# Agent attention with a mixture of experts: the marking of tokens that need their own answer, and the checked columns of the next batch

## The chip, the cores and the metric

The kernel runs on one core of one Trainium2 chip. The metric is the device time of one execution in microseconds (us). Two kernels are told apart here by medians of several executions. The engines are called as in the profile: PE multiplies matrices (PEld loads its weights), DVE, ACT and POOL work on vectors, and SP only issues transfers between device memory and the chip's own memory, one after the other in the order of its queue.

## The reference

Four batches of 11456 tokens with 128 values each go through attention over 49 agents per batch. The result of that is routed, token by token, to the one of 8 experts whose embedding is nearest, and gated.

```python
def sm(a, b):
    s = scale * (a @ b.transpose(0, 2, 1))
    s = s - s.max(-1, keepdims=True)
    e = np.exp(s)
    return e / (e.sum(-1, keepdims=True) + 1e-09)
agent_v = sm(agents, k) @ v
x = (sm(q, agents) @ agent_v).reshape(B * S, D)
...
logits = xn @ en.T / tau
expert_idx = np.argmax(logits, axis=1)
gate_w = probs[np.arange(N), expert_idx]
for e in range(E):
    mask = expert_idx == e
    h = np.maximum(x[mask] @ w1[e], 0.0)
    out[mask] = gate_w[mask, None] * (h @ w2[e])
```

## The kernel before, in words

The kernel does each batch in units of 8 columns of 128 tokens. A first pass over k and v builds the batch's agent values; a second pass over q computes scores, weights, routing and the answer. Nearly all tokens of a batch go to one expert, so the kernel picks that expert per batch (`pick_expert`) and computes its answer for all tokens in one cheap form: a linear part (`yp` from `lin`, L1275) plus two blocks of hidden columns (`hp`, `hh`, `hl`, and `yp` from `w2p`, L1284 to L1286), added up in PSUM. DVE multiplies the finished `yp` by the gate into a tile `ot` (L1299), and SP writes that to the output (L1306). There are three `ot` tiles; a fourth one waits until the transfer of the first has landed.

The cheap form treats most hidden columns as always on or always off. The hidden columns nearest to a change of sign are the checked columns: `pick_expert` gathers them into `vm` at its very end (L936), and `proved` (L1127 to L1133) multiplies every token with them and keeps a minimum and a sum. `mark_strays(b)` then finds the tokens whose answer is not covered: those whose own expert is another one, whose scale is out of bounds, or whose check failed. It builds a one-hot of the best expert (`oh`), its index (`idx`), bounds (`odd`, `ne`), the candidate list (`mine`), waits until all columns are checked, and takes the top candidates of each partition (`top`, `some`, `had`, `mput`), all as small DVE steps with a few PE products between. Up to 128 of a batch's marked tokens are answered exactly by `fix(b)`, which loads an expert's weights (`w1s`, `w2s`, L945 and L946), gathers the tokens, computes (`sqT`, `ssp`, `seT`, `sx`, `shp`, `syp`) and scatters the answers into the output (L1396). Left-over tokens are counted and handled in a loop (`stray`).

The program is written by Python generators that take turns; `yield n` hands over for n turns. `mark_strays(b)` is started when the last group of the batch is routed, and `fix(b)` waits until `vm` of the next batch exists. What the generators write is not yet the order of an engine: a scheduler places each instruction by when it expects the data and the engine, among those written nearby. Each engine then runs its own list strictly in order, and SP's list too: a transfer that waits (for its data, or for the transfer eight places earlier in the list, whose completion semaphore it uses) holds up all behind it. In batch 3, where no batch follows, marking and fixing run as urgent work at the end.

Of the kernel before, what the change touches and what calls it, by code (L numbers as in the profile page):

```python
# [11 lines left out]
F32 = mybir.dt.float32  # L12
# [3 lines left out]
ALU = mybir.AluOpType  # L16
AX = mybir.AxisListType
ROP = bass.bass_isa.ReduceOp

P = 128  # L20
# [10 lines left out]
def kernel(ctx: ExitStack, tc: tile.TileContext, q, k, v, agents, emb, tau, w1, w2, out):  # L31
    nc = tc.nc
    pe, dve, act, pool, sp = nc.tensor, nc.vector, nc.scalar, nc.gpsimd, nc.sync

    B, N, C = q.shape
    A = agents.shape[1]
    E, D, F = w1.shape
# [14 lines left out]
    NCOL = J + REM_J  # L52
# [30 lines left out]
    sm = ctx.enter_context(tc.tile_pool(name="sm", bufs=2))  # L83
# [208 lines left out]
    down = cst.tile([P, E], F32, name="down")  # L292
# [93 lines left out]
    batches = [Obj() for _ in range(B)]  # L386
# [659 lines left out]
    def route_group(b, gi, n):  # L1046
# [67 lines left out]
        if gi == len(groups) - 1:  # L1114
            spawn(mark_strays(b) if b < B - 1 else urgent(mark_strays(b), 4), 1, half=True)
# [27 lines left out]
    def mark_strays(b):  # L1143

        bt = batches[b]
        while bt.groups < len(groups):
            yield 1
        odd = sm.tile([P, NCOL], F32, name="odd", tag="odd", bufs=1)
        ne = sm.tile([P, NCOL], F32, name="ne", tag="ne", bufs=1)
        dve.tensor_tensor(out=ne, in0=bt.l, in1=bt.l, op=ALU.mult)  # L1150
# [2 lines left out]
        yield 1  # L1153
        ga = gate_all[:, b, :]
        dve.tensor_scalar(ga, bt.es, 1e-9, None, ALU.add)
        oh = bt.lg
        dve.scalar_tensor_tensor(out=oh, in0=bt.lg, scalar=0.0, in1=down.unsqueeze(1).broadcast_to([P, NCOL, E]),
                                 op0=ALU.is_equal, op1=ALU.mult)
        yield 1
        dve.reciprocal(ga, ga)  # L1160
        yield 1
        idx = sm.tile([P, NCOL], F32, name="idx", tag="idx", bufs=1)
        dve.tensor_reduce(out=idx, in_=oh, axis=AX.X, op=ALU.max)
        yield 1
        dve.tensor_scalar(ne, idx, bt.e0, None, ALU.not_equal)
        yield 1
# [23 lines left out]
        for i in range(KEEP):  # L1190
# [5 lines left out]
                          in1=had[:, :KEEP].unsqueeze(2).broadcast_to([P, KEEP, P]), op=ALU.is_equal)  # L1196
# [505 lines left out]
    with nullcontext():  # L1702
        due = []
        for i in range(len(ticks) + LAG):
            if i < len(ticks):
                b, t, r = ticks[i]
# [12 lines left out]
            while due and due[0][0] <= i:  # L1719
                _, b, t, f = due.pop(0)  # L1720
# [44 lines left out]
```

## Time and profile before

| | before |
|---|---|
| median of 3 runs | 677.67 us (677.25 to 678.22) |
| profiled execution, own time | 679.16 us |
| its span, from first to last instruction | 677.4 us |
| mean granted TensorE clock | 0.986 |
| PE busy | 632.3 us, 93% of the span |
| DVE busy | 525.1 us, 78% |
| ACT busy | 478.3 us, 71% |
| POOL busy | 317.7 us, 47% |
| transfers on the main queue | 68.8% of 16 engines' span |

The own time of the profiled execution is 1.49 us above the median of the runs and 1.8 us above its span. PE is the busiest engine by far; its idle time, and the stretches in which it was granted half of its clock, are what the other engines and the transfers cost.

### The profile page before, as it was taken

The page shows a single profiled execution, that of the slowest core. Times are in us where ns is not written, and L with a number is a line of the kernel's source. Part 1 is how long each engine was busy: PE and PEld are TensorE (multiplying, and loading weights), DVE is VectorE, ACT ScalarE, POOL GpSimd, SP SyncE. Part 2 cuts the span into 40 slices and gives each one's busy share as a digit, 9 for nine tenths or more (in the row PEclk, how much of TensorE's full clock was granted, in tenths as well). Part 3 has the DMA queues.
Part 4 walks back from the last instruction along what each step waited for, and adds up shares of the span by engine and source line. Part 5 has one row for each costly group of instructions (what it writes and reads, how often), then busy time and mean ns, then how long its engine had stood idle before and what let it go on. Part 6 is the DMA issues. An engine that isn't in the chain of part 4 may idle for free. (4 is left out here: it accounts for less than half of the span.)

```text
span 677.4 us, 23627 instructions
## 1 busy us (share of the span) xinstructions
PE 632.3 (93%) x9309; PEld 524.3 (77%) x9309; DVE 525.1 (78%) x1483; ACT 478.3 (71%) x1362; POOL 317.7 (47%) x588
## 2 busy tenths in 40 slices
PE   8998999999998899999999797999999999999995
PEld 6887788778886787888877586687887778887784
DVE  4757988867678999776779985986576999958992
ACT  3556589887689757887779753876657974888831
POOL 6000455375406536874524412677463356867300
PEclk9998999999999999999999997999999999999998
DMA  8998389989986399797986277739585534244121
GB/s 338 295 302 298 117 191 253 216 189 276 227 213 158 101 218 265 188 233 205 289 251 152 78 151 204 182 101 265 138 251 159 141 104 129 49 112 129 64 97 41
DMA packets 163138, 124.81 MB, mean 184 GB/s; under 512 B 82860, under 2 KB 139264, under 8 KB 163026
## 3 DMA queue, kind: packets, MB, share of 16 engines
q1 hardware_dynamic: 162706, 123.01, 68.8%
q8 instruction: 74, 1.21, 0.7%
q0 software_dynamic: 320, 0.27, 0.2%
q14 instruction: 38, 0.31, 0.1%
HBM read 80.26 MB, written 23.79 MB: 154 GB/s over the span
## 5 line engine op out<-in xcount | busy, mean ns | idle before, releaser
L1261 DVE SCALAR_TENSOR_TENSOR hl<-hp,hh 128x512 f16<-128x512 f32 (+1 forms) x184 | 122.3, 667 | 30.9 <-ACT hh L1260 30.1
L1284 PE MATMUL yp<-w2p,hh 128*128 128x128 f16 x720 | 137.4, 219 | 3.1 <-ACT hh L1260 2.9
L1285 PE MATMUL yp<-w2p,hh 128*128 128x128 f16 x720 | 136.8, 219 | 0.0
L1131 ACT ACTIVATE under<-vp 128x304 f16<-128x304 f32 (+1 forms) x268 | 114.8, 429 | 29.2 <-PE vp L1127 25.2
L1260 ACT ACTIVATE hh<-hp 128x512 f16<-128x512 f32 (+1 forms) x184 | 107.4, 589 | 37.9 <-PE hp L1257 29.4
L1286 PE MATMUL yp<-w2p,hl 128*128 128x128 f16 x720 | 133.6, 219 | 0.4 <-DVE hl L1261 0.4
L440 ACT COPY fT<-fTp 128x512 f32<-128x512 f32 (+1 forms) x136 | 75.4, 574 | 28.7 <-PE fTp L433 18.6
L1127 PE MATMUL vp<-vm,tt 128*128 128x304 f16 x360 | 93.0, 293 | 1.9 <-ACT under L1131 0.5
L451 PEld LDWEIGHTS sp<-aT_all,fT 128*64 128x64 f32 x2336 | 78.9, 139 | 17.5 <-issue 7.8
L451 PE MATMUL sp<-aT_all,fT 128*64 128x49 f32 x2336 | 89.4, 226 | 1.7 <-ACT fT L440 0.6
L1284 PEld LDWEIGHTS <-hh 128*128 128x128 f16 x720 | 71.3, 99 | 17.8 <-ACT hh L1260 5.7
L994 POOL TENSOR_TENSOR e<-qe,e 128x392 f16<-128x392 f32 (+1 forms) x46 | 40.5, 880 | 84.4 <-ACT e L993 80.8
L1286 PEld LDWEIGHTS <-hl 128*128 128x128 f16 x720 | 71.0, 99 | 11.2 <-issue 1.5
L1299 DVE TENSOR_TENSOR ot<-yp,gs 128x512 f32<-128x512 f32 (+1 forms) x92 | 61.5, 670 | 17.9 <-DMA out_dram<-ot 9.2
L1285 PEld LDWEIGHTS <-hh 128*128 128x128 f16 x720 | 70.8, 98 | 5.3 <-issue 0.5
L1256 PE MATMUL hp<-tt,gh 128*128 128x512 f16 (+1 forms) x184 | 69.0, 376 | 3.2 <-ACT under L1131 1.3
L1275 PE MATMUL yp<-lin,tt 128*128 128x128 f16 x720 | 62.6, 220 | 8.1 <-DVE ot L1299 7.8
L1078 POOL TENSOR_TENSOR nrm<-qq,half 128x16 f32<-128x16 f32 (+2 forms) x28 | 69.8, 2492 | 0.0
L1257 PE MATMUL hp<-tt,gl 128*128 128x512 f16 (+1 forms) x184 | 68.9, 375 | 0.0
L1275 PEld LDWEIGHTS <-tt 128*128 128x128 f16 x720 | 48.9, 99 | 13.4 <-issue 4.9
L1131 ACT ACTIVATION_READ_ACCUMULATOR under<-vp 128x1 f32 (+1 forms) x268 | 55.4, 207 | 0.0
L433 PE MATMUL fTp<-ident,qt 128*128 128x128 f32 (+1 forms) x344 | 54.5, 281 | 0.7 <-ACT under L1131 0.3
(366 smaller groups left out, 1513.4 us busy)
## 6 DMA issues: line engine op xcount, KB each, us to landing
kt<-in_k_dram SPq DMA_DIRECT2D x44, 512.0 KB, 7.0
vt<-in_v_dram SPq DMA_DIRECT2D x44, 512.0 KB, 5.7
out_dram<-ot SPq DMA_DIRECT2D x88, 256.0 KB, 2.7
qt<-in_q_dram SPq DMA_DIRECT2D x42, 512.0 KB, 6.1
w1s<-in_moe_w_dram SPq DMA_DIRECT2D x9, 512.0 KB, 4.1
w2s<-in_moe_w_dram SPq DMA_DIRECT2D x9, 512.0 KB, 8.2
q<-in_q_dram SPq DMA_DIRECT2D x2, 512.0 KB, 11.0
tt<-e SPq DMA_TRANSPOSE x46, 3.1
```

The lines of the kernel that those rows point to most:

```text
L440: act.copy(dst, tp[:, : m * p])
L451: i = pe.matmul(out=s[h : h + w, c * A : (c + 1) * A], lhsT=xT[:, c * p + h : c * p + h + w], rhs=rhs, start=True, stop=True, skip_group_c ...
L1078: pool.tensor_tensor(out=nrm, in0=quad, in1=half[:, :n], op=ALU.pow)
L1127: pe.matmul(out=z[:p, :FV], lhsT=tts[b, u][:, c * p : (c + 1) * p], rhs=bt.vm, start=True, stop=True)
L1131: act.activation(under[:p], z[:p, :FV], AF.Relu, scale=-1.0, accum_out=bt.vsum[:p, at])
L1256: pe.matmul(out=hp[:, :m], lhsT=bt.gh[:, fs], rhs=tt, start=True, stop=False)
L1260: h_last[:] = [act.activation(hh[:, :m], hp[:, :m], AF.Relu)]
L1261: dve.scalar_tensor_tensor(out=hl[:, :m], in0=hp[:, :m], scalar=0.0, in1=hh[:, :m], op0=ALU.max, op1=ALU.subtract)
L1275: pe.matmul(out=yp[:p, c, :], lhsT=tc_, rhs=bt.lin[:, h], start=(c == 0 and h == 0), stop=False, skip_group_check=True)
L1284: pe.matmul(out=y, lhsT=hh[:, cs], rhs=wh, start=False, stop=False, skip_group_check=True)
L1285: pe.matmul(out=y, lhsT=hh[:, cs], rhs=wl, start=False, stop=False, skip_group_check=True)
L1286: y_last[:] = [pe.matmul(out=y, lhsT=hl[:, cs], rhs=wh, start=False, stop=last, skip_group_check=True)]
```

## The change

In `mark_strays`, the one-hot `oh` and the index `idx` are written first, as soon as all groups of the batch are routed. For batches 0 to 2 a wait follows in the writing order, until the next batch's `vm` has been written, and two turns more; the bounds, the candidates, the top search, the scatter positions, the gates and the counts are written after it. For batch 3 only the order of the first steps changes. No instruction is added or taken away.

```diff
         while bt.groups < len(groups):
             yield 1
+        oh = bt.lg
+        dve.scalar_tensor_tensor(out=oh, in0=bt.lg, scalar=0.0, in1=down.unsqueeze(1).broadcast_to([P, NCOL, E]),
+                                 op0=ALU.is_equal, op1=ALU.mult)
+        yield 1
+        idx = sm.tile([P, NCOL], F32, name="idx", tag="idx", bufs=1)
+        dve.tensor_reduce(out=idx, in_=oh, axis=AX.X, op=ALU.max)
+        yield 1
+        if b < B - 1:
+            while not hasattr(batches[b + 1], "vm"):
+                yield 1
+            yield 2
         odd = sm.tile([P, NCOL], F32, name="odd", tag="odd", bufs=1)
         ne = sm.tile([P, NCOL], F32, name="ne", tag="ne", bufs=1)
         dve.tensor_tensor(out=ne, in0=bt.l, in1=bt.l, op=ALU.mult)
...
         dve.tensor_scalar(ga, bt.es, 1e-9, None, ALU.add)
-        oh = bt.lg
-        dve.scalar_tensor_tensor(out=oh, in0=bt.lg, scalar=0.0, in1=down.unsqueeze(1).broadcast_to([P, NCOL, E]),
-                                 op0=ALU.is_equal, op1=ALU.mult)
-        yield 1
         dve.reciprocal(ga, ga)
-        yield 1
-        idx = sm.tile([P, NCOL], F32, name="idx", tag="idx", bufs=1)
-        dve.tensor_reduce(out=idx, in_=oh, axis=AX.X, op=ALU.max)
         yield 1
```

After the change, lines from about L1176 on stand 4 lines lower (L1306 is L1310, L1192 is L1196). The listings below are of what the scheduler made of each program.

The first place is where the next batch's `vm` is made, in the marking of batch 1. This is SP's list there, before: the loads `vt` (v of the next pass) and `w2s` (weights for `fix`), the transpose `kT`, another `vt`, then the outputs of finished `ot` tiles.

```order
L159 DMA vt_8418<-in_v_dram 128x8x128
L946 ISA
L946 DMA w2s_8523<-in_moe_w2_dram 128x8x128
L555 DMA_TRANSPOSE kT_8361<-ks_8124 128x16x128
L159 DMA vt_8544<-in_v_dram 128x8x128
L1306 DMA out_0_dram<-ot_8407 128x512
L1306 DMA out_0_dram<-ot_8563 128x512
L1306 DMA out_0_dram<-ot_8671 96x256
L1306 DMA out_0_dram<-ot_8778 128x512
```

And the same place of SP's list after the change:

```order
L159 DMA vt_8406<-in_v_dram 128x8x128
L159 DMA vt_8521<-in_v_dram 128x8x128
L555 DMA_TRANSPOSE kT_8354<-ks_8121 128x16x128
L1310 DMA out_0_dram<-ot_8396 128x512
L946 ISA
L946 DMA w2s_8577<-in_moe_w2_dram 128x8x128
L1310 DMA out_0_dram<-ot_8536 128x512
L1310 DMA out_0_dram<-ot_8666 96x256
L1310 DMA out_0_dram<-ot_8768 128x512
```

The second `vt` has moved ahead of the transpose, the first output stands right behind the transpose, and `w2s` has moved from ahead of the transpose to behind that output. On DVE the same place reads so before, with `vm`, the `ot` that needs the first of these outputs landed, and the marking's `had` and `mput`:

```order
L936 TENSOR_SCALAR vm_7312<-placed_8235,thr_8206 128x304
L1299 TENSOR_TENSOR ot_8778<-yp_8707,gs_8108 128x512
L982 TENSOR_REDUCE qmx_8332<-sp_8315 128x8
L985 TENSOR_TENSOR qe_8334<-sp_8315,qmx_8332 128x392
L1192 TENSOR_SCALAR had_8358<-iotaf_147,had_8379 128x3
L1195 TENSOR_TENSOR mput_8416<-iotaf_147,had_8358 128x384
```

And after the change:

```order
L1303 TENSOR_TENSOR ot_8768<-yp_8703,gs_8106 128x512
L936 TENSOR_SCALAR vm_7312<-placed_8224,thr_8199 128x304
L982 TENSOR_REDUCE qmx_8328<-sp_8311 128x8
L985 TENSOR_TENSOR qe_8330<-sp_8311,qmx_8328 128x392
L1265 SCALAR_TENSOR_TENSOR hl_8736<-hp_8732,hh_8735 128x512
L421 TENSOR_TENSOR m_run_6104<-sp_8376,m_run_6104 128x392
L1036 TENSOR_TENSOR rt_8426<-rtp_8409,qe_8005 128x392
L1074 TENSOR_REDUCE rmx_8527<-rtg_8156 128x16
L1265 SCALAR_TENSOR_TENSOR hl_8787<-hp_8783,hh_8786 128x512
L1303 TENSOR_TENSOR ot_8940<-yp_8800,gs_8106 128x512
L1133 TENSOR_REDUCE vmin_7890<-vp_8790 128x1
L1041 TENSOR_REDUCE qq_7767<-rt_8426 128x2x8
```

`had` and `mput` follow two rows later, so they move eight rows down. The marking up to the top search of batch 1 (`idx`, `ne`, `odd`, `mine`, `top`, spread over some 60 rows that end about 30 rows above `vm`) stands in the same rows of DVE in both programs, ahead of `vm`; in batch 0 only a pair or two of neighbouring rows is swapped. Up to here all engines have otherwise the same order in both programs.

The second place is the scatter of batch 1's `fix`, again on SP. Before, the transpose `tt` and then an output that waits for the scatter:

```order
L946 DMA w2s_9286<-in_moe_w2_dram 128x8x128
L1005 DMA_TRANSPOSE tt_9256<-e16_0_142 128x8x128
L1306 DMA out_0_dram<-ot_9109 128x512
L1306 DMA out_0_dram<-ot_9258 128x512
L159 DMA vt_9511<-in_v_dram 128x8x128
L159 DMA qt_9531<-in_q_dram 128x1024
```

After, the output that answers to `ot_9109` (`ot_9093`) stands thirteen rows ahead of the first output that waits for the scatter, and that one (`ot_9248`) stands behind three loads:

```order
L1005 DMA_TRANSPOSE tt_9246<-e16_0_142 128x8x128
L159 DMA vt_9507<-in_v_dram 128x8x128
L946 ISA
L946 DMA w2s_9371<-in_moe_w2_dram 128x8x128
L159 DMA qt_9531<-in_q_dram 128x1024
L159 DMA vt_9642<-in_v_dram 128x8x128
L1310 DMA out_0_dram<-ot_9248 128x512
```

So the scatter comes later against the outputs, and what waits for it comes one `ot` later. At batch 2's `fix` it is the same: one output that stood behind the scatter before stands ahead of it now.

The third place is the end of PE's list, in `fix(3)`. Before, everything after the last `yp` product:

```order
L1286 LDWEIGHTS hl_14029
L1286 MATMUL yp_14047<-w2p_10692,hl_14029 96x128
L228 MATMUL mB_13608<-ident_84,mTx_13606 128x32
L1347 MATMUL ssp_13702<-aT_all_118,sxT_13700 128x49
L1359 MATMUL seT_13741<-ident_84,se_13715 49x128
L1368 MATMUL sx_13754<-seTs_13743,av_all_137 128x128
```

After the change `mB` and `ssp` stand 64 rows earlier, between `yp` products, with 32 products behind them:

```order
L1289 MATMUL yp_14004<-w2p_10692,hh_13949 128x128
L228 MATMUL mB_13608<-ident_84,mTx_13606 128x32
L1351 MATMUL ssp_13702<-aT_all_118,sxT_13700 128x49
L1290 LDWEIGHTS hl_13950
...
L1290 MATMUL yp_14047<-w2p_10692,hl_14029 96x128
L1363 MATMUL seT_13741<-ident_84,se_13715 49x128
L1372 MATMUL sx_13754<-seTs_13743,av_all_137 128x128
```

`seT` is now the first instruction after the last `yp` product, and the DVE steps between `ssp` and `seT` (L1350 and L1353) stand ahead of the last two `ot`.

## Rows read from the trace of the kernel before

**Rows 1.** The page's first part: engine, busy us, share of span, instructions.
```profile
PE 632.3 (93%) x9309; PEld 524.3 (77%) x9309; DVE 525.1 (78%) x1483; ACT 478.3 (71%) x1362; POOL 317.7 (47%) x588
```

**Rows 2.** Windows: from:to, length, busy us (instructions) per engine, granted clock, DMA share, GB/s.
```profile
400.00:420.00 20.00, 15.81 (x223) 13.43 (x220) 12.18 (x30) 7.14 (x15) 3.94 (x11) 0.83 0.84 196
420.00:660.00 240.00, 230.93 (x3272) 190.33 (x3272) 197.76 (x570) 173.39 (x547) 132.58 (x215) 1.00 0.51 141
```

**Rows 3.** Waits from 340 to 660 us: total us, times, longest.
```profile
DVE ot L1299 <- DMA out_dram<-ot: 9.2, 5, 5.2
...
PE yp L1275 <- DVE ot L1299: 7.4, 5, 4.2
```

**Rows 4.** Timeline of PE, 404 to 420 us: start, duration, instruction, [idle before, releaser].
```profile
404.92 0.61 PE L1275 MATMUL yp<-lin,tt 128*128 128x128 f16 x8
...
406.55 1.14 PE L451 MATMUL sp<-aT_all,fT 128*64 128x49 f32 x32
...
413.11 1.04 PE L1275 MATMUL yp<-lin,tt 128*128 128x128 f16 x8 [4.19 <-DVE ot L1299]
...
415.78 1.95 PE L451 MATMUL sp<-aT_all,fT 128*64 128x49 f32 x32
```

**Rows 5.** Timeline of DVE, 404 to 420 us.
```profile
406.66 0.53 DVE L936 TENSOR_SCALAR vm<-placed,thr 128x304 f16<-128x304 f32 x1 [0.61 <-PE placed L866]
412.36 0.69 DVE L1299 TENSOR_TENSOR ot<-yp,gs 128x512 f32<-128x512 f32 x1 [5.17 <-DMA out_dram<-ot]
```

**Rows 6.** Timeline of SP, 396 to 420 us: start of issue, its duration.
```profile
399.56 7.08 SPq L555 DMA_TRANSPOSE kT<-ks  x1
406.69 0.58 SPq L159 DMA_DIRECT2D vt<-in_v_dram  x1
407.37 6.04 SPq L1306 DMA_DIRECT2D out_dram<-ot  x4
```

**Rows 7.** Tile out_dram, 370 to 440 us: from issue to landing; page, part 6: sizes and medians.
```profile
DMA to landing us min/median/max: 2.0/2.6/4.7
...
vt<-in_v_dram SPq DMA_DIRECT2D x44, 512.0 KB, 5.7
```

**Rows 8.** Windows as in rows 2, around the stall and around an earlier, shorter one.
```profile
386.00:388.00 2.00, 0.83 (x9) 0.42 (x7) 2.00 (x6) 0.00 (x0) 1.86 (x4) 1.00 0.88 235
388.00:392.00 4.00, 4.00 (x27) 2.79 (x27) 3.43 (x21) 1.39 (x6) 0.89 (x4) 0.57 0.09 37
...
408.00:412.00 4.00, 0.92 (x16) 0.68 (x13) 0.00 (x0) 1.31 (x3) 0.00 (x0) 1.00 0.95 290
412.00:420.00 8.00, 6.89 (x81) 6.03 (x81) 6.36 (x18) 2.58 (x6) 2.24 (x9) 0.57 0.40 97
```

**Rows 9.** Timelines of PE, stalls of 1.0 to 1.4 us.
```profile
355.04 0.75 PE L451 MATMUL gp<-avT,w1s 128*64 128x49 f32 x18 [1.36 <-DMA w1s<-in_moe_w_dram]
...
387.41 0.33 PE L433 MATMUL fTp<-ident,kt 128*128 128x128 f32 x1 [1.03 <-DVE vmin L1133]
...
461.85 0.61 PE L1275 MATMUL yp<-lin,tt 128*128 128x128 f16 x8 [1.06 <-DVE ot L1299]
...
610.42 0.55 PE L1275 MATMUL yp<-lin,tt 128*128 128x128 f16 x7 [1.38 <-DVE ot L1299]
```

**Rows 10.** Timelines of POOL, SP and DVE: the scatter of batch 1 and what waits for it.
```profile
454.31 1.09 POOL L1396 DMA_INDIRECT out_dram<-so,ix  x1 [0.75 <-DVE so L1393]
...
459.04 0.84 SPq L1306 DMA_DIRECT2D out_dram<-ot  x2
...
461.10 0.69 DVE L1299 TENSOR_TENSOR ot<-yp,gs 128x512 f32<-128x512 f32 x1 [2.12 <-DMA out_dram<-ot]
```

**Rows 11.** Timeline of PE at the end, and one full-speed row of the same product.
```profile
446.55 1.16 PE L1382 MATMUL shp<-sx,w1s 128*128 128x128 f32 x8
...
663.62 0.31 PE L1359 MATMUL seT<-ident,se 128*49 128x128 f32 x1 [1.01 <-ACT se L1356]
...
665.12 3.51 PE L1382 MATMUL shp<-sx,w1s 128*128 128x128 f32 x16 [0.35 <-ACT sx L1371]
```

## The prediction

> **What bounds the kernel now.** The first view is the page's list of engines: PE is busy for 632.3 of 677.4 us [rows 1], so a change that adds no work can give back at most PE's idle time and the time PE spent at half clock. The second view is the table of windows. From 420 to 660 us PE is busy for 230.93 of 240 us at full clock [rows 2]: some 9 us to win or lose by, in small pieces. The stretch from 400 to 420 us stands out, with 15.81 us busy and a mean clock of 0.83. The list of waits names its cause: of the 9.2 us in which `ot` waited for a landed output, 5.2 came at once, and of the 7.4 us that PE's `yp` waited for `ot`, 4.2 [rows 3]. The timelines show the chain. SP issues the transpose `kT` from 399.56 on and is held in it for 7.08 us; only then come a 512 KB `vt` at 406.69 and, at 407.37, the outputs [rows 6]. DVE, which had nothing left to do before it, could write the next `ot` only at 412.36 [rows 5], and PE started at 413.11 after 4.19 us idle [rows 4]. Thereafter PE ran at half clock: the eight `yp` products took 1.04 us instead of 0.61, the 32 `sp` products 1.95 instead of 1.14 [rows 4].
>
> **What the change does there.** No instruction is added, so no engine has more work. The waiting in the writing order does not reach the engines: the listings show the marking up to `top` still ahead of `vm` in batch 0 and 1. I therefore cost not "marking after `vm`", but what did move. Before `vm` of batch 2, at about 407 us, the orders agree, so the first 400 us should repeat. Five terms follow, gain positive.
>
> *Term 1, the stall at 408.9 us.* In the new list the first output stands right behind `kT`; the `vt` that was between them is now ahead of `kT`, where `w2s` stood. Both are 512 KB, so `kT` still has two loads ahead of it and should be done issuing at the same time, about 406.7. The output is then issued 0.68 us earlier (406.69 instead of 407.37, [rows 6]), and 512 KB (0.524 MB) that had to move ahead of it are gone. From 408 to 412 us 290 GB/s were moved [rows 8], so these bytes stood for 1.8 us. Sum: 2.5 us. As a check, this output had the slowest landing of its stretch, 4.7 us against a median of 2.6 [rows 7]; 2.6 us after 406.69 would be 409.3, a gain of 3.1. Bounds: 0.7, if only the issue slot is saved, and 4.2, if the stall is gone. I take 2.5, which leaves PE 1.7 us idle.
>
> *Term 2, the half clock behind the stall.* From 412 to 420 us the mean clock is 0.57 [rows 8], that is 6.9 us at half clock, of which 5.8 fall behind PE's restart at 413.11. By the ratio of the two `yp` rows (1.04 to 0.61, a factor of 1.7) this cost 5.8 x (1 - 1/1.7) = 2.4 us. For a shorter stall the trace has two answers. After idle times of 1.36, 1.06 and 1.38 us the clock stayed up; around the 1.03 us at 387.41 [rows 9] PE was busy for only 0.83 of 2 us, and the next 4 us had a mean clock of 0.57 [rows 8], or 3.4 us at half, which cost 1.4 us. A stall of 1.7 us is nearer to the latter, so I take 2.4 - 1.4 = 1.0; bounds 0 (same stretch) and 2.4 (none). The Trainium skill (TensorE: Matmul & The Clock Gate, HAM oscillation) reckons the penalty of a throttled stretch as half its length, which for 5.8 us would be an estimated 2.9 us; the rows give 2.4, and I keep the rows.
>
> *Term 3, the end.* After PE's last `yp`, the chain `ssp`, `smx`, `se`, `seT` was run in the open, and `seT` waited 1.01 us for `se` [rows 11]. Now `ssp` has 32 products behind it, some 2 us (eight take 0.61 us from the first start to the last end, [rows 4]), and its DVE steps stand ahead of the last two `ot`. The wait goes: 1.0. Bounds: 0.5, if half of it reappears in front of `seT`; 2.2, if the shorter gap also keeps the clock up, since the sixteen `shp` products took 3.51 us against 1.16 for eight at full speed [rows 11].
>
> *Term 4, batch 2's scatter, about 610 us.* PE waited 1.38 us for an `ot` whose tile was tied to an output behind the scatter [rows 9]. One output now goes ahead of the scatter, and the `ot` that waits comes later, about one unit `yp` later against the end of `fix`. I take 0.7; bounds 0 and 1.4.
>
> *Term 5, batch 1's scatter, about 461 us.* Here PE waited 1.06 us [rows 9]: the scatter was issued at 454.31, the outputs behind it at 459.04, and `ot` was written at 461.10 [rows 10]. In the new list one output has gone ahead, but the next one stands behind `w2s`, `qt` and a `vt`, so the wait moves rather than goes; and a cluster of products `avp` now stands close together in PE's list near there. I charge 0.6; bounds +0.5 and the case below.
>
> Everything else (the counts, the stray work of DVE, the loads, none of which is needed soon after it is issued) moves by a few rows against other work; I take 0 for it, with 1.5 either way, since the 240 us from 420 on hold only some 9 us of idle time. What hides the marking's steps is DVE's own slack; DVE is busy for 78% [rows 1] and these steps stay in number.
>
> Sum: 2.5 + 1.0 + 1.0 + 0.7 - 0.6 = 4.6 us, against the profiled execution's 679.16, that is 674.6 there. That execution stood 1.5 us above the median of the runs; from the median of 677.67 the same 4.6 us give **673.1 us**.
>
> **The rivals.** *B: the output lands as late as before.* If the 4.7 us of the slow landing come from how busy the transfer engines are (share 0.95 from 408 to 412 us, [rows 8]) and not from the `vt` ahead of it, then `w2s`, which now follows the output directly, makes it as slow. Only the issue slot remains: 0.7 + 0 + 1.0 + 0.7 - 0.6 = 1.8, or 675.9, and about 677 if the tail gives nothing. For it: the share is high through the whole stall. Against it: the other outputs landed in 2.6 us, some of them between loads too. The Trainium skill speaks to both sides (DMA: Bandwidth & Descriptors): in "Queues, rings and completion order" each engine takes its descriptors in ring order, which is for the forecast, and in "Latency and other measured facts" memory latency grows tenfold under load, to 2 us, which is for B.
>
> *C, slower: the load queue in front of batch 1's late output.* In the new list the output that waits for the scatter has three loads of 512 KB directly ahead. If these have not started to move when the scatter lands, 1.57 MB at 290 GB/s [rows 8] put 5.4 us on PE's wait, and a stall of this length brings a half-clock stretch as in term 2, 2.4 us: 4.6 + 0.6 - 7.8 = -2.6, or 680.3. It turns slower by 0.2% when more than 6 us of these 7.8 come true, so nearly all three loads must still be in front. For it: SP is strictly in order, and `w2s` can be issued only when `syp` is done. Against it: the scatter lands some 4 us after its issue [rows 10], in which time the loads can have moved.
>
> *D: nothing to be measured.* The marking did not move up to `top`; the few swaps may shift each wait to the next `ot`, with terms 1, 4 and 5 cancelling: 677.7, or up to 1.5 us more.
>
> **How the numbers follow.** About 0.2%, 1.4 us, is what a measurement of this kernel can tell from no change: faster is below 676.3, slower above 679.0. The forecast has 0.60, with a range of its own from 670.6 (terms 1 and 2 near their upper bounds) to 675.5; B has 0.18, half of it below 676.3; C 0.12; D 0.10, of which 0.03 are slower. Faster: 0.58 + 0.09 = 0.67; same: 0.02 + 0.09 + 0.07 = 0.18; slower: 0.12 + 0.03 = 0.15. From 670.3 to 678.6 all but about 2 in 10 is held: some 0.07 lie below (terms 2 and 3 both at their upper bounds), 0.13 above (C, and the slow end of D).
>
> **What the changed profile would show.** Term 1: the longest wait of `ot` for an output, near 408 us, between 2 and 3.5 us instead of 5.2, PE's idle time before that `yp` 1 to 2.5 us, and the output issued right after `kT`. Term 2: a mean clock from 400 to 420 us above 0.83, about 0.9. Term 3: no wait in front of `seT`, and the span ending about 1 us earlier after the last `yp`. Terms 4 and 5: `yp` waits for `ot` of under 0.8 us near 606 us and about 1.5 near 458. Wrong would be: a `kT` issue that takes longer than 7.08 us (the first `vt` not gone by then), a new wait of some us between 408 and 470 us, or a stall that only moves on to the next `ot`, behind `w2s`.

## The result, and the profile after

The change did not make the kernel faster; both comparisons came out slower. The first (four executions of each) gave 687.18 us against 677.94, a ratio of 1.0104 [1.0064 to 1.0145]. Run once more, twelve executions against 35 of the kernel before, it gave 681.70 against 678.70, a ratio of 1.0031 [0.9999 to 1.0063]. (The ratios leave out executions more than 1.5% behind the fastest of their kernel, and they are not the quotient of the medians shown, which would be 1.0044 here.) Executions of one kernel spread wider than three runs of before had shown: 677.87 to 688.33 for the change, 675.75 to 686.26 for before, and the first four lay from near the middle of that range to just above its top. The loss is thus 0.3 to 1.0%, 2 to 7 us (the repeat by itself only just leaves no change possible); 673.1 us was forecast, with a range up to 678.6.

| | after, first profile (684.2 us) | after, second profile (678.4 us) | before [rows 1] |
|---|---|---|---|
| own time of that execution | 686.03 us | 680.13 us | 679.16 us |
| mean granted clock | 0.978 | 0.994 | 0.986 |

The engines have the same work as before; the page of the first profile:

```profile
PE 635.7 (93%) x9309; PEld 528.2 (77%) x9309; DVE 525.3 (77%) x1483; ACT 480.3 (70%) x1362; POOL 317.9 (46%) x588
```

To see where the time went, I cut each trace at the starts of the same `ot` writes of DVE (the 46th, 48th, 56th, 78th and 92nd in its list). The table has each piece's length and PE's idle time in it, in us, as before / second profile / first profile; the times at its left are those of before.

| piece | length | PE idle |
|---|---|---|
| up to 403.6 | 403.6 / 403.1 / 406.6 | 23.4 / 26.6 / 23.9 |
| 403.6 to 420.6 (terms 1, 2) | 17.0 / 13.4 / 13.6 | 4.2 / 2.3 / 2.3 |
| 420.6 to 477.8 (term 5) | 57.2 / 64.0 / 65.1 | 3.0 / 5.8 / 6.5 |
| 477.8 to 619.0 (term 4) | 141.2 / 141.7 / 142.7 | 5.5 / 7.3 / 7.1 |
| 619.0 to 662.1 | 43.1 / 44.5 / 44.4 | 0.6 / 1.5 / 1.4 |
| 662.1 to the end (term 3) | 15.3 / 11.7 / 11.9 | 8.4 / 7.1 / 7.3 |

From the second line on the lengths add up to a loss of 1.5 us in the second profile and 3.8 in the first. A single length also changes when work moves from one piece to its neighbour (of the 6.8 us by which the third line's piece grew in the second profile, some 2.5 are neither idle time nor half clock, but products that moved into it), so I read a term from the idle time and from the half clock.

In the first line PE and ACT have the same order in both programs, SP has it up to the loads ahead of `kT`, and DVE and POOL differ in swapped neighbours of the marking, from about 227 us on. Windows of the first profile (columns as in [rows 2]) show where it lost 3.0 us: not by idle time (0.5 us more), but in stretches at half clock that before does not have. Two of them:

```profile
200.00:220.00 20.00, 18.16 (x280) 15.10 (x277) 17.14 (x57) 17.58 (x45) 11.22 (x22) 0.91 0.65 154
260.00:280.00 20.00, 19.81 (x275) 16.25 (x273) 17.60 (x60) 15.45 (x55) 12.97 (x23) 0.91 1.03 254
```

A third lies at 360 us. The second profile, of the same program, has no such stretch in its first 400 us, so the swaps do not bring them by themselves. That the swaps make them likelier is not excluded: between 200 and 370 us, five of the nine profiles with the new writing order (this one, nowait, b1, pin and after_ot4 of the experiments below) have a granted clock below 1.00, and none of the five without it. The second profile's windows also answer to [rows 2]: the stall at 408 us shrank, and a new loss stands behind it.

```profile
0.00:400.00 400.00, 373.45 (x5751) 310.11 (x5752) 311.60 (x864) 295.85 (x794) 180.02 (x362) 1.00 0.83 216
400.00:420.00 20.00, 17.19 (x262) 14.81 (x260) 13.33 (x30) 8.92 (x22) 6.27 (x12) 0.91 0.93 233
420.00:480.00 60.00, 54.81 (x760) 44.56 (x756) 44.97 (x144) 42.22 (x137) 36.91 (x59) 0.97 0.70 180
```

Before, the last of these had PE busy for two us more, at full clock:

```profile
420.00:480.00 60.00, 57.00 (x813) 46.80 (x813) 47.95 (x145) 44.31 (x144) 38.93 (x60) 1.00 0.70 188
```

The list of waits of the first profile, 400 to 660 us, answers to [rows 3]. The longest wait of PE for `ot` fell from 4.2 to 2.6 us, but `rtp` now waits 2.8 us in all for its transpose `tt`, 0.3 before, and `avp` for `qe` is new:

```profile
DVE ot L1303 <- DMA out_dram<-ot: 9.4, 3, 4.1
...
PE yp L1279 <- DVE ot L1303: 6.0, 3, 2.6
PE rtp L1016 <- DMA tt<-e: 2.8, 3, 1.2
...
PE avp L600 <- DVE qe L985: 1.2, 1, 1.2
```

SP's timeline at the stall answers to [rows 6]. The output stands right behind `kT`, as the order said, and `w2s` behind it:

```profile
403.55 6.65 SPq L555 DMA_TRANSPOSE kT<-ks  x1
410.31 0.53 SPq L1310 DMA_DIRECT2D out_dram<-ot  x1
411.02 0.38 SPq L946 DMA_DIRECT2D w2s<-in_moe_w_dram  x1
```

DVE and PE there, against [rows 4, 5]: `ot` is written 2.87 us after that issue (413.18 - 410.31; before 412.36 - 407.37 = 4.99), and PE waits 2.09 us instead of 4.19.

```profile
413.18 0.69 DVE L1303 TENSOR_TENSOR ot<-yp,gs 128x512 f32<-128x512 f32 x1 [4.14 <-DMA out_dram<-ot]
```

```profile
413.92 0.27 PE L1279 MATMUL yp<-lin,tt 128*128 128x128 f16 x2 [2.09 <-DVE ot L1303]
```

The scatter of batch 1 answers to [rows 10]. On SP four loads are issued around it, and then nothing until it has landed:

```profile
460.42 0.57 SPq L159 DMA_DIRECT2D vt<-in_v_dram  x1
461.23 0.44 SPq L946 DMA_DIRECT2D w2s<-in_moe_w_dram  x1
461.72 1.26 SPq L159 DMA_DIRECT2D qt<-in_q_dram  x1
463.02 0.43 SPq L159 DMA_DIRECT2D vt<-in_v_dram  x1
467.95 1.91 SPq L1310 DMA_DIRECT2D out_dram<-ot  x3
```

On POOL, the scatter and the time from its issue to its landing (4.7 us before):

```profile
461.93 1.10 POOL L1400 DMA_INDIRECT out_dram<-so,ix  x1 [0.28 <-DVE qq L1041]
...
DMA to landing us min/median/max: 6.0/6.0/6.0
```

So the outputs go out at 467.95, which is 461.93 + 6.0, and `ot` follows 3.87 us later (2.06 before: 461.10 - 459.04). On DVE and on PE:

```profile
471.82 0.69 DVE L1303 TENSOR_TENSOR ot<-yp,gs 128x512 f32<-128x512 f32 x1 [2.93 <-DMA out_dram<-ot]
```

```profile
466.98 1.10 PE L600 MATMUL avp<-vt,kd 128*64 128x129 f32 x16 [1.22 <-DVE qe L985]
...
472.56 0.80 PE L1279 MATMUL yp<-lin,tt 128*128 128x128 f16 x8 [2.55 <-DVE ot L1303]
```

PE idles twice within 6 us, and the eight `yp` products behind it take 0.80 us instead of 0.61 [rows 9]: a half-clock stretch, in the second profile too (0.97 over 60 us above). At the end, against [rows 11], the wait before `seT` is gone, and the sixteen `shp` products run at full clock, 2.05 us instead of 3.51:

```profile
672.03 0.27 PE L1363 MATMUL seT<-ident,se 128*49 128x128 f32 x1
...
673.49 2.05 PE L1386 MATMUL shp<-sx,w1s 128*128 128x128 f32 x16 [0.36 <-ACT sx L1375]
```

### The profile page after: what moved, and what is told of

Same layout as the page of the kernel before. It is cut to its first block, busy times and chain, and to the rows that moved or that the text cites. A ratio compares the mean times of both kernels' runs of the same rounds, so it can differ in the third digit from the quotient of the medians.

```text
span 684.2 us, 23612 instructions
## 1 busy us (share of the span) xinstructions
PE 635.7 (93%) x9309; PEld 528.2 (77%) x9309; DVE 525.3 (77%) x1483; ACT 480.3 (70%) x1362; POOL 317.9 (46%) x588
## 5 line engine op out<-in xcount | busy, mean ns | idle before, releaser
L1288 PE MATMUL yp<-w2p,hh 128*128 128x128 f16 x720 | 139.3, 221 | 1.9 <-ACT hh L1264 1.9
L1289 PE MATMUL yp<-w2p,hh 128*128 128x128 f16 x720 | 139.0, 221 | 0.0
L1290 PE MATMUL yp<-w2p,hl 128*128 128x128 f16 x720 | 135.7, 221 | 0.0
L451 PEld LDWEIGHTS sp<-aT_all,fT 128*64 128x64 f32 x2336 | 81.2, 143 | 17.7 <-issue 7.7
L451 PE MATMUL sp<-aT_all,fT 128*64 128x49 f32 x2336 | 92.0, 229 | 1.7 <-ACT fT L440 0.6
L1039 POOL TENSOR_TENSOR rt<-rt 128x384 f32<-128x384 f32 (+1 forms) x48 | 40.4, 841 | 32.4 <-DVE rt L1036 30.5
```

Of the source, the lines that this page charges most:

```text
L451: i = pe.matmul(out=s[h : h + w, c * A : (c + 1) * A], lhsT=xT[:, c * p + h : c * p + h + w], rhs=rhs, start=True, stop=True, skip_group_c ...
L1288: pe.matmul(out=y, lhsT=hh[:, cs], rhs=wh, start=False, stop=False, skip_group_check=True)
L1289: pe.matmul(out=y, lhsT=hh[:, cs], rhs=wl, start=False, stop=False, skip_group_check=True)
L1290: y_last[:] = [pe.matmul(out=y, lhsT=hl[:, cs], rhs=wh, start=False, stop=last, skip_group_check=True)]
```

## The experiments

Twelve runs in three groups; those of a group share their runs of the kernel before (median 678.70, 678.88 and 678.55 us).

| run | median us (runs) | ratio to before, 95% |
|---|---|---|
| again | 681.70 (12) | 1.0031 [0.9999 to 1.0063] |
| nowait | 678.61 (12) | 1.0017 [0.9978 to 1.0056] |
| b1 | 684.25 (12) | 1.0058 [1.0027 to 1.0090] |
| b2 | 679.07 (12) | 0.9985 [0.9955 to 1.0015] |
| pin | 684.67 (7) | 1.0091 [1.0057 to 1.0126] |
| prio | 671.98 (6) | 0.9891 [0.9858 to 0.9923] |
| after_ot4 | 680.50 (12) | 1.0022 [1.0002 to 1.0042] |
| before_ot4 | 676.53 (12) | 0.9970 [0.9951 to 0.9990] |
| ldahead | 689.34 (6) | 1.0155 [1.0122 to 1.0188] |
| ae | 679.30 (12) | 1.0002 [0.9976 to 1.0029] |
| aprio | 676.80 (12) | 0.9964 [0.9940 to 0.9988] |
| best1 | 678.18 (12) | 0.9986 [0.9957 to 1.0016] |

### Which part of the change does it

*again* is the changed kernel once more.

> The changed kernel once more, five rounds beside the kernel before. Theory P (place): the loss lies where the order differs, after 408 us: about 5 us around 460 to 480 (an `ot` that waits for an output, then a half-clock stretch) and about 4 us around 590 to 630 (three waits of `rtp` for the transpose `tt`, another `ot` wait, a half-clock stretch), so the median stays near 683 to 688 and these waits return in the profile. Theory Q (chance of the clock): 3.7 of the 6.8 us of the first profile were lost before the first changed row, in half-clock stretches at 214 and 260 us that the order does not explain; if those come and go, the runs spread over several us here and so do those of the kernel before, and the difference of the medians falls to 3 to 6 us.

*nowait* writes the one-hot and the index first, without the wait. Its lists on PE, ACT and SP are those of before; DVE and POOL have the swapped neighbours.

```diff
-        if b < B - 1:
-            while not hasattr(batches[b + 1], "vm"):
-                yield 1
-            yield 2
```

> Only the first half of the change: one-hot and index first, without the wait for the next batch's checked columns. PE, ACT and SP have the same order as before, DVE some swapped neighbours in each batch's marking. Theory P: as before within 0.2%. Rival R: the swaps near 213 us and 330 us cost something by themselves (the 3.7 us lost ahead of the first changed row), so 680 to 682.

*b1* and *b2* have the wait for one batch only.

```diff
-        if b < B - 1:
+        if b == 1:
```

> The wait for batch 1 alone. Its order is that of the changed kernel up to the marking of batch 2. Theory P: the stall at 409 us shorter by 2 to 3 us, the loss at 460 to 480 us there, those at 590 to 630 us gone or smaller: +1 to +4 us, about 679 to 682. If the loss sits in batch 2's part: 675 to 678.

> The wait for batch 2 alone. Its order is that of before up to the marking of batch 2, near 550 us. Theory P: the stall of 4.2 us at 409 us and the small one at 462 us as before, the `tt` waits and the stall at 620 us of the changed kernel there if they come from batch 2's own move: +2 to +4 us, about 680 to 682; if they come from the shifted order of batch 1, as before within 0.2%. The end (seT without its wait) may give 1 to 3 us back.

Without the wait the time is that of before, with an interval up to 0.6% above it, so the order of `oh` and `idx` is worth nothing that these runs can tell. With a wait for batch 0 alone the scheduler makes the same lists as without any, so that wait does nothing either (seen in the lists; not run). The wait of batch 1 carries both the gain at 408 us (PE idle for 2.4 us in that piece instead of 4.2) and the loss behind it (idle for 5.8 instead of 3.0, and for 6.8 instead of 5.5 between 478 and 619 us), with a lower clock. Its median lies above the 679 to 682 us that I had expected:

```profile
420.00:480.00 60.00, 54.31 (x723) 43.81 (x721) 44.80 (x145) 41.09 (x131) 37.03 (x57) 0.94 0.71 186
```

The wait of batch 2 carries the gain at the end (a last piece of 11.7 us, as after) and a loss between 478 and 619 us (143.8 us against 141.2); in sum nothing that can be measured. b1 and b2 together, +0.58 and -0.15%, make +0.43, within the interval of the whole change.

### What costs the time behind the stall, and what the stall was worth

*pin* is the changed kernel with its three loads `vt`, `qt`, `vt` tied behind the first output that waits for the scatter, so that they no longer stand in front of it.

```diff
+        if hasattr(batches[1], "fixed") and not hold:
+            hold[:] = [o_]
...
-            with in_place(w_last if b == 0 or now[0] // 2 < start + 2 else t_last):
+            pin = bool(hold) and len(held) < 3
+            if pin:
+                held.append(1)
+            with in_place(hold if pin else w_last if b == 0 or now[0] // 2 < start + 2 else t_last):
```

> The changed kernel with three loads (`vt`, `qt`, `vt`) tied to stand behind the first output that waits for the scatter of batch 1, as they did before; the rest of the list as changed up to there. Theory L (loads beside the scatter): in the three profiles of the changed order the scatter landed 5.7 to 6.0 us after its issue, with four 512 KB loads issued around it; without it 4.1. If the loads cause it, the scatter lands in about 4 us here, the `ot` wait that cost PE 2.4 to 2.6 us near 468 us falls under 1 us and the half-clock stretch there goes: 2 to 4 us less than the changed kernel's 681.7, so 678 to 680. Rival S (the scatter itself comes late in POOL's list): the wait stays above 2 us, 681 to 683.

The scatter landed in 3.0 us instead of 6.0, and from its issue (461.33) to PE's next `yp` it took 6.8 us, against 10.6 in the changed kernel (472.56 - 461.93) and 7.5 before (461.85 - 454.31): so the loads do make that chain longer. PE's wait did not go, because in the list of this kernel PE stands ready for that `yp` 3.8 us after the scatter's issue (468.17 - 3.01 - 461.33), against 8.1 in the changed kernel and 6.5 before:

```profile
DMA to landing us min/median/max: 3.0/3.0/3.0
```

```profile
468.17 0.61 PE L1279 MATMUL yp<-lin,tt 128*128 128x128 f16 x8 [3.01 <-DVE ot L1303]
...
572.97 0.19 PE L1016 MATMUL rtp<-r_hi,tt 128*128 128x58 f16 x1 [1.18 <-DVE w2p L907]
```

The second row is a wait that the changed kernel does not have. That the later loads brought it is not shown: ae below, with its loads in place, has one like it (1.57 us). The piece from 478 to 619 us grew to 148.9 us, and the time that I had hoped for was missed. pin settles the landing, not what it is worth. *prio* leaves the marking as before and only moves the output of [rows 6] ahead of `qt`, `vt` and `kT` (the scheduler then also put `w2s` behind `kT`):

```diff
-        sp.dma_start(out=dst, in_=o[:p, :n])
+        with tc.high_priority(400) if (b, t) in [(1, 20)] else nullcontext():
+            sp.dma_start(out=dst, in_=o[:p, :n])
```

> The kernel before, with one transfer moved: the output that the 4.2 us stall at 409 us waits for is issued ahead of the two loads and the transpose `kT` in front of it. Orders agree up to there, and little moves after it. Theory G (the gain at 409 us is that output's place alone, and has nothing to do with the marking): PE's wait there falls from 4.2 to 4.7 us to under 1, the half-clock stretch behind it gets shorter or goes, nothing is lost at 462 us: 3 to 6 us faster, 673 to 676. Rival: the next `ot` waits instead, for the output behind `kT`, `w2s` and `vt`: 2 to 4 us idle a few us later, and 676 to 679.

PE no longer waits there, the clock stays up, and in the 60 us behind it PE is as busy as before:

```profile
400.00:420.00 20.00, 19.60 (x333) 16.50 (x330) 17.86 (x55) 10.87 (x30) 9.80 (x16) 1.00 1.17 258
420.00:480.00 60.00, 57.13 (x771) 47.36 (x769) 45.77 (x126) 44.14 (x142) 36.31 (x58) 1.00 0.76 179
```

6.9 us were won, about the upper bounds of terms 1 and 2 together (4.2 + 2.4). This kernel beats both. *after_ot4* and *before_ot4* give `ot` a fourth tile, with room taken from two small tiles:

```diff
-        o = wk.tile([P, TJ, D], F32, name="ot", tag="ot", bufs=3)
+        o = wk.tile([P, TJ, D], F32, name="ot", tag="ot", bufs=4)
```

> The changed kernel with a fourth `ot` tile (two small tiles of the stray work share or lose a second copy to make room); the scheduler places other things too. Theory W (late outputs cost PE time only through the ring of three `ot` tiles): the waits of `yp` for `ot`, 2.2 at 410, 2.4 at 468 and 1.3 at 616 us, go or fall under 0.5 each, and with them two half-clock stretches: 674 to 678. Rival: the cost is in the crowded stretch itself (`avp` behind `qe`, `rtp` behind `tt`), and no more than 2 us come back: 679 to 682.

> The kernel before with a fourth `ot` tile in the same way. Theory W: the 4.2 us stall at 409 us and the half clock behind it go, 672 to 675, and the kernel stays ahead of the changed one with four tiles by no more than 2 us. Rival: the wait moves to the next `ot` and the scheduler uses the room otherwise: 676 to 679.

In both the wait for `ot` at 410 us was gone, but the scheduler dealt its lists anew and other waits came, so neither got what the wait had been worth. One of after_ot4:

```profile
560.14 0.19 PE L1016 MATMUL rtp<-r_hi,tt 128*128 128x58 f16 x1 [1.80 <-DVE w2p L907]
```

### Loads in front, or the place behind the scatter

*ldahead* takes the kernel before and puts three loads ahead of its first output behind the scatter.

```diff
-        sp.dma_start(out=s[:p, :n, :D], in_=src)
+        with tc.high_priority(400) if (kind, b, u) in [("v", 3, 7), ("q", 2, 9), ("v", 3, 8)] else nullcontext():
+            sp.dma_start(out=s[:p, :n, :D], in_=src)
```

> The kernel before with three loads (`vt`, `qt`, `vt`, 512 KB each) moved ahead of the first output that waits for the scatter of batch 1, where the changed kernel has them; SP's list differs in these rows alone, PE's from just behind the place. Theory L (loads beside the scatter delay it): the scatter lands 5.5 to 6 us after its issue instead of 4.1 to 4.7, the output behind it 1 to 2 us later, and PE's wait for `ot` near 462 us grows from 0.7 to 1.1 us to 2 to 3, with a half-clock stretch behind it in some runs: 679 to 682. Rival (the loads move beside other work in any case, PE's list is what makes the wait): the wait stays near 1 us, and the time within 0.2% of before.

This is the mechanism of rival C by itself, and costs more than the 679 to 682 us that I had expected. One half of that expectation failed: the scatter was not delayed. It had been issued at 452.52, 3.6 us ahead of the first of the three loads, and landed in 4.1 us. The scatter's landing, then SP's timeline, DVE's and PE's:

```profile
DMA to landing us min/median/max: 4.1/4.1/4.1
```

```profile
456.09 0.57 SPq L160 DMA_DIRECT2D vt<-in_v_dram  x1
456.71 0.63 SPq L160 DMA_DIRECT2D qt<-in_q_dram  x1
457.44 0.43 SPq L160 DMA_DIRECT2D vt<-in_v_dram  x1
458.00 8.56 SPq L1307 DMA_DIRECT2D out_dram<-ot  x4
```

```profile
465.50 0.69 DVE L1300 TENSOR_TENSOR ot<-yp,gs 128x512 f32<-128x512 f32 x1 [3.93 <-DMA out_dram<-ot]
```

```profile
466.25 1.01 PE L1276 MATMUL yp<-lin,tt 128*128 128x128 f16 x8 [4.97 <-DVE ot L1300]
```

The output behind the loads took 7.5 us (465.50 - 458.00) until its tile was free; the median of such outputs was 2.6 [rows 7], and the one at this place before took 2.06. The 5.4 us between them are what rival C put on three loads. PE idles for 7.8 us in the piece behind the stall instead of 3.0. The Trainium skill (DMA: Bandwidth & Descriptors, "Queues, rings and completion order") has each transfer engine take its descriptors in ring order; these rows agree with it.

*ae* takes the changed kernel and issues one output of batch 2 four turns sooner, so that it stands ahead of the scatter.

```diff
-        yield 5
+        yield 1 if (b, t) in [(2, 3)] else 5
```

> The changed kernel with one output, the one that waits for the scatter of batch 1, written four turns earlier, so that it stands ahead of the scatter on SP; the lists agree up to there. Theory C (that output behind the scatter is the stall): the wait of 2.4 to 2.6 us near 468 us falls to 1 us or less (the next output still waits for the scatter) and the half-clock stretch there goes in most runs: 2 to 4 us less than the changed kernel's 681.7, so 678 to 680. Rival (the next `ot` waits as long): 681 to 683.

With the loads and the scatter as they were (it landed in 5.3 us), the wait near 468 us is gone and the half-clock stretch with it. The wait of `avp` is gone too. PE idles for 2.5 us in that piece, less than before (3.0). The median is 2.4 us below again's, but the two intervals overlap, so this rests on the trace. Some of the gain was given back between 478 and 619 us (8.4 us idle against 7.3).

```profile
420.00:480.00 60.00, 57.55 (x798) 46.16 (x796) 48.16 (x152) 45.28 (x147) 38.73 (x61) 1.00 0.71 188
```

*aprio* is the changed kernel with prio's edit, *best1* is prio with an output ahead of the scatter by ae's edit, at (2, 2).

> The changed kernel with the output of the 409 us stall issued ahead of the transpose `kT` and its loads, as was done to the kernel before. PE's wait of 2.2 us there goes to 0 and with it one half-clock stretch. The lists behind it are dealt anew. Theory G: 3 to 5 us less than the changed kernel, 677 to 679, still 5 to 8 us behind the kernel before with the same edit (672), since the loss near 465 us and near 615 us stays. Rival: the lead of the other was luck of the order, and this one is at 672 to 675.

> The kernel before with both edits: the output of the 409 us stall ahead of `kT`, and one output of batch 2 written four turns earlier, ahead of the scatter of batch 1. Of the 672.0 of the first edit alone, the wait of 0.7 us near 455 us can go: 670.5 to 672. Rival: the list behind is dealt anew and gives 2 to 5 us back, 674 to 677.

With the edit of prio in both, the wait for the output near 409 us is out of the way, and aprio against prio gives a rough price of the rest of the change: 0.9964 against 0.9891 is 0.7%, some 5 us (from their intervals, 2 to 8; the two ran in different groups, and their lists differ elsewhere too). The 676.8 us are just below the 677 to 679 expected. Its PE still waits at the scatter:

```profile
468.24 0.61 PE L1279 MATMUL yp<-lin,tt 128*128 128x128 f16 x8 [2.21 <-DVE ot L1303]
```

best1 lost most of what prio had won: the lists behind the moved output were dealt anew, with new waits of 1.2 and 1.4 us near 456 and 462 us. It was meant to beat prio and did not. So a second moved output cost some 6 us, with the order behind it dealt anew: a difference of this size cannot be put down to the edited row alone without a look at the traces.

## Why the prediction was wrong

**The step that failed** is term 5, which charged 0.6 us for batch 1's scatter; 4 to 5 us were lost there. PE idled 2.8 us more (3.5 in the first profile), and the half-clock stretch behind it, 0.97 over 60 us or 3.6 us at half, cost 3.6 x (1 - 1/1.7) = 1.5 by term 2's ratio. The order had shown the cause, an output that waits for the scatter with three loads ahead of it; I priced it as rival C at 7.8 us, and gave it a chance of 0.12. The mechanism is C's, the size some 60% of it, and C's time of 680.3 us is near the repeat's 681.7. C's time is near by luck in part: its 7.8 us were 3.5 too many, and the gains that it kept beside them 1.9 too many.

What I held against C was that the loads can move while the scatter lands. They did in part, but not for nothing: the scatter took 6.0 us instead of 4.7, the output 3.87 instead of 2.06 (not the 7.5 of ldahead), together 3.1 us more. Of the signs that were to show the forecast wrong, one came: a new wait of some us between 408 and 470 us. PE stood ready at 470.01 (472.56 - 2.55); with the 7.5 us of before it could have started at 461.93 + 7.5 = 469.4, without a wait. ldahead shows that loads directly ahead of the output delay it in the old order as well, pin how the scatter lands without them, and ae that the loss goes when the output stands ahead of the scatter. The new wait of `avp` (1.2 us) stands at the products that I had seen move together there and had not priced; it is gone in ae and pin, and no run took it apart.

**Terms 1 and 2** came out in size: 3.5 us forecast, 1.9 by idle time and 1.3 by the clock measured ((6.8 - 3.6) x (1 - 1/1.7)), together 3.2. PE idled 2.1 us in front of that `yp` (1.7 forecast) and the clock was 0.91 (about 0.9 forecast). Rival B fell: with `w2s` right behind it, the output's tile was free after 2.87 us. Two parts of the working did not hold. The output was not issued 0.68 us earlier: `kT` began 1.0 us later against the cut at 403.6 (3.05 us ahead of it in the first profile, 4.05 before), and the output came 3.7 us behind the cut, where it was 3.8 before. The whole gain is the faster landing, 2.1 us (4.99 - 2.87) where 1.8 were forecast. And the length of the stall does not by itself set the half clock behind it: ldahead has 0.91 in this window too, after 4.45 us idle. So the size of term 2 is luck in part.

**Term 3** was mis-sized: 1.0 us forecast, 1.1 to 1.3 by idle time and 1.5 by `shp` at full clock (3.51 - 2.05) measured, 2.6 to 2.8 in all, above my upper bound of 2.2. That the shorter gap might keep the clock up I had counted as a bound only. It did in all seven profiles whose list ends in the new way: `shp` took 2.05 us and the last piece 11.7 to 12.1. The seven with the old end have 2.05 to 3.57 us and 13.6 to 15.4; nowait, with the same list on PE as before, took 13.7 and not 15.3, so some of the gain is a slow end of the profiled execution of before.

**Term 4** had the wrong sign: +0.7 us forecast, 1.6 to 1.8 us more idle time measured (1.3 more in b1, 0.8 in b2, so more of it comes with the shifted order of batch 1 than with batch 2's own). In the first profile PE still waited 1.31 us for `ot` there, about as long as before, and new is a wait of 1.19 us for the transpose `tt`, which SP issued only at 614.53; half clock followed (eight `yp` in 1.04 us):

```profile
618.16 0.20 PE L1016 MATMUL rtp<-r_hi,tt 128*128 128x58 f16 x1 [1.19 <-DMA tt<-e]
...
620.32 1.04 PE L1279 MATMUL yp<-lin,tt 128*128 128x128 f16 x8 [1.31 <-DVE ot L1303]
```

**"Everything else 0, 1.5 either way"** held in size, but all to one side: 0.8 to 0.9 us more idle from 619 to 662 us, in further waits of `rtp` for `tt`.

In sum, for the repeat: 3.2 - 4.3 - 1.8 - 0.9 + 2.8 = -1.0 us from the first changed row on (by the lengths -1.5), against +4.6 forecast; the medians differ by 3.0. **The measurement's resolution** was taken wrong as well. I took 0.2%, from three runs within 1 us. Twelve runs against 35 leave 0.3% either way, since executions of one program lie up to 10 us apart. The first result's further loss is not shown to be the change's: 3.0 us of its profile were lost ahead of the moved transfers, in half-clock stretches that come and go.

## What to carry to other kernels

Where a scheduler places the instructions, a change in the writing order is a change of the transfer queue: follow every output against the loads and scatters around it, and cost the worst one in full, with the half clock behind it, before adding up the gains. When one transfer is late, move that transfer: prio won with one line twice what the change was worth at its best place, while PE idled 0.9 us more in the two pieces behind it. Then look at the whole list again: best1 moved one output more and lost most of it. Where stalls are short and the clock falls after some of them, three runs are no error bar; take a dozen before believing half a per cent.

## What the runs showed of the hardware

Half-clock stretches come at different places in executions of one program: 0.91 at 200 and 260 us in one profile of the changed kernel, none before 400 us in the other. The scatter landed in 3.0 us with the loads tied behind the next output, in 4.1 (ldahead) and 4.7 us (before) in the old order, and in 5.3 us (ae) and 6.0 (the change) with four loads issued around it. An output directly behind three loads of 512 KB freed its tile in 7.5 us (ldahead), against 2.06 without them (before).

After a stall of 2.09 to 2.17 us the stretch at half clock was about half as long as after one of 4.19: (1 - 0.91) / 0.5 x 20 = 3.6 us against 6.8 for the same window of before (0.83, [rows 2]). It is no rule: in ldahead PE idled 4.45 us there, and the window has 0.91.

```profile
411.67 0.69 PE L1276 MATMUL yp<-lin,tt 128*128 128x128 f16 x8 [4.45 <-DVE ot L1300]
```

```profile
400.00:420.00 20.00, 15.55 (x247) 13.63 (x245) 13.11 (x35) 6.60 (x16) 4.86 (x12) 0.91 0.86 204
```
